# A decode step of attention and SwiGLU on one core: the loop over KV groups gets a ninth pass, both K blocks of a group go ahead of the V blocks, and most of the output projections use 512-column matmuls

## The chip, the cores and the metric

The kernel runs on one core of a Trainium2 chip. The metric is the device time of one execution in microseconds (us). Three runs gave 354.53, 354.72 and 354.78 us; the median is 354.72 us.

The core's engines run side by side and wait for each other on semaphores: TensorE (PE in the profile; PEld is its weight load), VectorE (DVE), ScalarE (ACT), GpSimd (POOL), and SyncE (SP), which here only issues transfers. Transfers from memory run on 16 DMA engines that the SP queue feeds.

## The reference

One token of width 512 goes through two branches, and a gate mixes them.

```python
q = (x @ wq)                                  # 32 heads of 128
k = repeat(k_cache, 4); v = repeat(v_cache, 4)  # 8 KV heads, 32768 keys of 128
p = softmax(q . k * 128 ** -0.5)
a = (p @ v).reshape(1, 1, 4096) @ wo          # 4096 -> 512
b = (silu(x @ w_gate) * (x @ w_up)) @ w_down  # 512 -> 1792 -> 512
g = sigmoid((x * gate_w).sum(-1))
return g * a + (1 - g) * b
```

Everything is bf16 in memory. The K and V caches are 8 x 32768 x 128 each, 67 MB apiece; wq and wo are 4.2 MB each, w_gate, w_up and w_down 1.8 MB each. Each byte of these is read once, 148 MB in all.

## The kernel before

**Tiles.** The 8 KV heads are called groups (G = 8, four query heads each). The 32768 keys of a group are cut into two blocks (NB = 2) of 16384 keys, 4 MB of K and 4 MB of V per block. On-chip memory has five pages of one block each: pages 0 and 2 take the K blocks (PG_K), pages 1 and 3 the V blocks (PG_V), page 4 (PG_X) holds wq at the start and wo at the end. Page 3 holds w_gate and w_up at first. w_down has a tile of its own, wd. This text writes K0(g), K1(g), V0(g), V1(g) for the blocks of group g.

**A K block on TensorE (emit_k, L403).** It is cut into eight units. For each unit eight fp32 transposes (L381, emit_fill) write the two PSUM tiles pst in turn; DVE copies a unit to the tile ktT (L641); 16 matmuls with the query (L393, emit_scores) write the scores to ps_sc, two units behind the transposes. After the last unit's scores DVE reduces the block's maximum (L646), and after both blocks POOL takes it over all partitions (L262). Each fill counts up sem_fill; when it has counted a whole block, that K page may be loaded anew.

**A V block on TensorE (emit_v, L428).** ACT has turned the group's scores into exponentials ET (L519). 32 matmuls with 512 columns (L440) add ET times V to ps_o, on four strips of 32 rows in turn. The last one counts up sem_v_free, and the V page is free. Ahead of block 0 stands emit_reduce (L415), eight recorded fp32 matmuls (L419) that fold the accumulator of an earlier group, which ACT copied out of PSUM (L531).

**The loop on TensorE (L450).** Eight passes, one per group. Pass g does K0(g), V0(g-1), K1(g), V1(g-1); the V blocks are skipped in pass 0. After the loop stand the V blocks of group 7, the sums of the exponentials (L470), a last emit_reduce, then w_down (emit_proj, 14 slices j with four 128-column matmuls each, one per strip), a matmul that permutes the attention output (L486), and wo (32 slices j, four matmuls each) into the same sums ps_c. DVE copies these out (L676) and SP writes the 512 outputs.

**The order of the loads (L266 on).** SP issues all large loads in one order, and a wait in front of one holds up all behind it: wq, w_gate, w_up, K0(0), K1(0), V0(0), K0(1), K1(1), V1(0), then for g from 2 to 7: K0(g), V0(g-1), K1(g), V1(g-1); then V0(7), V1(7), w_down, and wo in five cuts (WO_CUTS). Each K load waits for the fills of the block that has its page, each V load for sem_v_free of the V block that has its page. One load is different: V1(7) goes to K page 0 with a semaphore of its own (sem_vl) and waits for the fills of K0(7).

Of the kernel before, what the change touches and what calls it, by code (L numbers as in the profile page):

```python
# [13 lines left out]
def bass_gated_mix__gqa_block_cached__swiglu_ffn__decode_kernel(  # L14
# [41 lines left out]
    SCALE = float(DH) ** -0.5  # L56
    assert UPG == STEP and UPP % NKT == 0 and UPP % NST == 0
    assert KC * H * DH <= PAGE and 2 * KC * F <= PAGE and WOJ * NOUT <= PAGE
    WO_CUTS = [0, 16, 24, 28, 30, 32]
    OC = NOUT // 128  # L60

    RQ = 4
# [10 lines left out]
    with ExitStack() as es:  # L73
        def S_(name):
            return es.enter_context(nc.semaphore(name))

        sem_page = [S_(f"s_page{i}") for i in range(4)]
        sem_vl = S_("s_vl")
# [32 lines left out]
        sem_dve_oT2 = S_("s_dve_oT2")  # L111
        sem_dve_O2 = S_("s_dve_O2")
        sem_dve_row = S_("s_dve_row")
        sem_act_g = S_("s_act_g")
        sem_act_sg = S_("s_act_sg")
        sem_nbias = S_("s_nbias")
# [8 lines left out]
        def T(name, shape, dt):  # L125
            return es.enter_context(nc.sbuf_tensor(name, shape, dt))
# [42 lines left out]
        oTs = T("oTs", [128, H], BF16)  # L169
        O2a = T("O2a", [128, WOJ], BF16)  # L170
        O2 = T("O2", [128, WOJ], BF16)
        res_row = T("res_row", [128, 128], BF16)

        def P(name, shape, dt):
# [13 lines left out]

        ps_e = pst[0][:, 0:512]
        ps_c = pst[1][:, 0:512]  # L190

        def row_view(p):
            return page[:, p, :].rearrange("p (r d) -> p r d", d=DH)
# [5 lines left out]
        with nc.Block("main") as block:  # L199
# [66 lines left out]
            @block.sync  # L266
            def _(sp):
                def cache(which, g, b, p, sem):
                    sp.dma_start(  # L269
                        page[:, p, :].rearrange("p (r d) -> p r d", d=DH),  # L270
                        which[0, g, b * BLK : (b + 1) * BLK, :].rearrange("(p r) d -> p r d", r=R),
                    ).then_inc(sem, 16)

                def load_k(g, b):
                    if g:
                        sp.wait_ge(sem_fill, UPG * (g - 1) + UPP * (b + 1))
                    cache(A_k_cache, g, b, PG_K[b], sem_page[PG_K[b]])

                def load_v(g, b):
                    p, sem = PG_V[b], sem_page[PG_V[b]]  # L280
                    if (g, b) == (G - 1, NB - 1):
                        p, sem = PG_K[0], sem_vl
                        sp.wait_ge(sem_fill, UPG * (G - 1) + UPP)
                    elif g:
                        sp.wait_ge(sem_v_free, NB * (g - 1) + b + 1)
                    elif PG_V[b] == PG_F:
                        sp.wait_ge(sem_pe_h, 1)
                    cache(A_v_cache, g, b, p, sem)

                sp.dma_start(wq_v, A_wq.rearrange("(p c) n -> p c n", c=KC)).then_inc(sem_q, 16)  # L290
                for w, src in enumerate((B_w_gate, B_w_up)):
                    sp.dma_start(  # L292
                        wgu[:, w, :, :], src.rearrange("(p c) f -> p c f", c=KC)
                    ).then_inc(sem_f, 16)
                for b in range(NB):
                    load_k(0, b)
# [10 lines left out]
                sp.dma_start(  # L307
                    wd[:, :, :], B_w_down.rearrange("(p j) n -> p j n", j=FC)
                ).then_inc(sem_ld_wd, 16)
# [12 lines left out]
            @block.tensor  # L322
            def _(pe):
# [101 lines left out]
                        )  # L425
                    ins.then_inc(sem_red, 1)

                def emit_v(i, b, last=False):  # L428
                    view = row_view(PG_K[0] if last else PG_V[b])
                    if b == 0:  # L430
                        emit_reduce(i)
                    if last:
                        pe.wait_ge(sem_vl, 16)
                    else:
                        pe.wait_ge(sem_page[PG_V[b]], i)
                    pe.wait_ge(sem_exp, i + 8 * (b + 1))
                    for k in range(R // RQ):
                        n = b * R + k * RQ
                        c = k % NSTRIP
                        ins = pe.matmul(  # L440
                            ps_o[32 * c : 32 * c + RQ * HPG, :],
                            ET[:, n : n + RQ, :].rearrange("p n h -> p (n h)"),
                            view[:, k * RQ : (k + 1) * RQ, :],
                            start=(b == 0 and k < NSTRIP),
                            stop=(b == NB - 1 and k >= R // RQ - NSTRIP),
                            skip_group_check=True,
                        )
# [8 lines left out]
                def emit_proj(w, vec, j, first, last):  # L456
                    for oc in range(OC):
                        ins = pe.matmul(  # L458
                            ps_c[32 * oc : 32 * oc + 1, 0:128],
                            vec[:, j : j + 1],  # L460
                            w[:, j, oc * 128 : (oc + 1) * 128],
                            start=first,
                            stop=last,
                            skip_group_check=True,
                        )
                    return ins

                emit_v(G * STEP, 0)
                pe.wait_ge(sem_dve_esum2, 1)
                pe.matmul(  # L470
                    ps_e[:, 0:H],
                    ones_f[:, :],
                    esum2[:, :, :].rearrange("p g h -> p (g h)"),
                    start=True,
                    stop=True,
                ).then_inc(sem_pe_S, 1)
                emit_v(G * STEP, 1, last=True)
                emit_reduce((G + 1) * STEP)
                pe.wait_ge(sem_dve_tT, 1)
                pe.wait_ge(sem_ld_wd, 16)  # L480
                for j in range(FC):
                    emit_proj(wd, tT, j, j == 0, False)

                pe.wait_ge(sem_dve_oT2, 1)
                pe.wait_ge(sem_dve_pm, 1)
                pe.matmul(  # L486
                    ps_m[:, M_O0 : M_O0 + WOJ], pmat[:, :], O2a[:, :], start=True, stop=True
                ).then_inc(sem_pe_O2, 1)
                pe.wait_ge(sem_dve_O2, 1)
                for k, s in enumerate(sem_wo):  # L490
                    pe.wait_ge(s, 16)
                    for j in range(WO_CUTS[k], WO_CUTS[k + 1]):
                        ins = emit_proj(wo_v, O2, j, False, j == WOJ - 1)
                ins.then_inc(sem_pe_sum, 1)

            @block.scalar
            def _(act):
# [44 lines left out]
            def _(dve):  # L542
# [162 lines left out]
```

## Time and profile before

| | |
|---|---|
| median of three runs | 354.72 us |
| the profiled execution | 354.56 us, of which the span 352.8 us |
| mean granted TensorE clock | 0.848 of full speed |
| busy: PE, PEld, DVE, ACT, POOL | 268.0, 233.3, 176.5, 32.3, 5.8 us |
| DMA | 148.26 MB, 420 GB/s over the span |
| K load, V load (16 each) | 4096 KB, 27.7 and 31.5 us from issue to landing (median) |
| SP waited for TensorE's transposes | 215.8 us in 14 waits |
| SP waited for TensorE's V matmuls | 75.0 us in 13 waits |

How to read it: the profile is of one execution. Time from issue to landing holds the time that a load stands in the queue behind earlier loads. SP's waits are not a cost in themselves: SP has nothing else to do. A line of the timeline gives start, length, engine, line, operation, tile written and tiles read, the count, and in square brackets the idle time before it with what ended it. Matmul ends are modelled.

### The profile page before, as it was taken

What the parts mean: (1) busy time and instruction counts of PE and PEld (TensorE: products, weight loads), DVE (VectorE), ACT (ScalarE), POOL (GpSimd) and SP (SyncE); (2) the same over time, 40 slices, a digit from 0 to 9 for tenths busy, and PEclk for the clock granted to TensorE, in tenths of its full rate; (3) what the DMA queues carried; (4) which work ended last, traced back from release to release, by engine and by line L of the source; (5) the groups of instructions that cost most, each with busy time, mean ns of one, the idle gap of its engine ahead of it and who ended that gap; (6) DMA issues with size and microseconds to landing.
All of it is one profiled execution on the core that took longest, in us unless ns stands there. A gap on an engine that the chain in (4) does not pass through costs nothing.

```text
span 352.8 us, 8863 instructions
## 1 busy us (share of the span) xinstructions
PE 268.0 (76%) x4093; PEld 233.3 (66%) x4093; DVE 176.5 (50%) x201; ACT 32.3 (9%) x148; POOL 5.8 (2%) x24
## 2 busy tenths in 40 slices
PE   0446986999897949796796959894997949695584
PEld 0446986978796939494775739593967849494243
DVE  1210977566692818375564719083654818192000
ACT  1000000400300040003000030004000030004000
POOL 0200000000000000000000000000000000000000
PEclk9999989698998987789898879589785978898655
DMA  8999999999999999999999999999999999999994
GB/s 327 414 432 433 440 422 404 431 427 438 431 431 424 446 428 424 424 450 427 427 424 450 424 427 427 446 424 427 427 446 424 427 436 435 431 424 438 408 423 165
DMA packets 5926, 148.26 MB, mean 420 GB/s; under 512 B 666, under 2 KB 668, under 8 KB 1052
## 3 DMA queue, kind: packets, MB, share of 16 engines
q1 hardware_dynamic: 5912, 148.12, 98.1%
q8 instruction: 7, 0.11, 0.1%
q14 instruction: 3, 0.02, 0.0%
q10 hardware_dynamic: 4, 0.00, 0.0%
HBM read 148.11 MB, written 0.00 MB: 420 GB/s over the span
## 4 chain that ended last, share of the span: by engine, by line
DMA 65%; PE 31%; DVE 2%; SPq 1%; issue 0%
DMA page<-in_A_k_cache_dram 53%; PE pst L381 23%; DMA page<-in_A_wo_dram 12%; PE ps_sc L393 5%; PE ps_o L440 2%; DVE ktT L641 2%; PE ps_m L419 1%; SPq L314 0%; SPq L292 0%; SPq L269 0%; SPq L307 0%; PE pst L458 0%; SPq L290 0%; DVE res_row L676 0%
## 5 line engine op out<-in xcount | busy, mean ns | idle before, releaser
L641 DVE COPY ktT<-pst 128x2048 bf16<-128x2048 bf16 x128 | 156.0, 1224 | 110.1 <-PE pst L381 103.1
L381 PE MATMUL pst<-ident_f,page 128*128 128x128 f32 x1024 | 158.7, 313 | 43.5 <-DMA page<-in_A_k_cache_dram 41.6
L381 PEld LDWEIGHTS pst<-ident_f,page 128*128 128x128 f32 x1024 | 135.8, 162 | 54.0 <-DMA page<-in_A_k_cache_dram 49.4
L393 PEld LDWEIGHTS ps_sc<-qcur,ktT 128*128 128x128 bf16 x2048 | 67.0, 97 | 11.4 <-DVE ktT L641 10.0
L393 PE MATMUL ps_sc<-qcur,ktT 128*128 128x8 bf16 x2048 | 67.8, 166 | 8.6 <-DVE ktT L641 8.6
L440 PE MATMUL ps_o<-page,ET 128*16 128x512 bf16 x512 | 41.3, 480 | 5.0 <-DMA page<-in_A_v_cache_dram 5.0
L440 PEld LDWEIGHTS ps_o<-page,ET 128*16 128x16 bf16 x512 | 13.2, 103 | 22.1 <-issue 9.9
L510 ACT ACTIVATE nbias<-gmax 128x4 f32<-128x4 f32 x8 | 1.6, 205 | 263.8 <-POOL gmax L262 263.8
L519 ACT ACTIVATE ET<-ps_sc,nbias 128x128 bf16<-128x128 f32 x64 | 24.1, 552 | 0.9 <-PE ps_o L440 0.3
L519 ACT ACTIVATION_READ_ACCUMULATOR ET<-ps_sc,nbias 128x1 f32 x64 | 18.0, 281 | 0.0
L646 DVE TENSOR_REDUCE pmaxf<-ps_sc 128x4 f32<-128x512 f32 x16 | 11.1, 692 | 10.4 <-PE ps_sc L393 10.4
L419 PE MATMUL ps_m<-sel,acc 128*128 128x4 f32 x72 | 11.6, 284 | 4.1 <-ACT acc L531 4.1
L419 PEld LDWEIGHTS ps_m<-sel,acc 128*128 128x128 f32 x72 | 10.9, 232 | 5.5 <-ACT acc L531 5.5
L366 PE MATMUL ps_m<-xT,page 128*128 128x1 bf16 x112 | 6.9, 198 | 5.2 <-DMA page<-in_B_w_up_dram 5.2
L366 PEld LDWEIGHTS ps_m<-xT,page 128*128 128x128 bf16 x112 | 6.8, 162 | 5.3 <-DMA page<-in_B_w_up_dram 5.3
L262 POOL PARTITION_ALL_REDUCE gmax<-pmax x8 | 3.0, 374 | 293.0 <-DVE pmax L648 293.0
L632 DVE COPY oT<-ps_m 128x4 f32<-128x4 f32 x8 | 1.3, 156 | 12.9 <-PE ps_m L419 12.9
L342 PE MATMUL ps_m<-xT,page 128*128 128x1 bf16 x128 | 3.6, 165 | 5.3 <-DMA page<-in_A_wq_dram 5.3
L342 PEld LDWEIGHTS ps_m<-xT,page 128*128 128x128 bf16 x128 | 3.5, 104 | 5.3 <-issue 5.3
L531 ACT ACTIVATE acc<-ps_o 128x512 f32<-128x512 f32 x8 | 5.2, 649 | 14.6 <-PE ps_o L440 14.6
L329 PE MATMUL ps_m<-ones_bf,x_row 1*128 1x1 bf16 x4 | 0.3, 172 | 7.8 <-DMA gw_row<-in_gate_w_dram 7.8
L458 PE MATMUL pst<-page,O 128*1 128x128 bf16 x128 | 4.3, 305 | 2.5 <-DMA page<-in_A_wo_dram 2.4
(62 smaller groups left out, 24.0 us busy)
## 6 DMA issues: line engine op xcount, KB each, us to landing
page<-in_A_k_cache_dram SPq DMA_DIRECT2D x16, 4096.0 KB, 27.7
page<-in_A_v_cache_dram SPq DMA_DIRECT2D x16, 4096.0 KB, 31.5
page<-in_A_wq_dram SPq DMA_DIRECT2D x1, 4096.0 KB, 12.7
page<-in_A_wo_dram SPq DMA_DIRECT2D x1, 2048.0 KB, 39.7
page<-in_B_w_gate_dram SPq DMA_DIRECT2D x1, 1792.0 KB, 16.5
page<-in_B_w_up_dram SPq DMA_DIRECT2D x1, 1792.0 KB, 21.3
wd<-in_B_w_down_dram SPq DMA_DIRECT2D x1, 1792.0 KB, 35.3
page<-in_A_wo_dram SPq DMA_DIRECT2D x1, 1024.0 KB, 41.8
```

The source lines that it names most:

```text
L262: pool.partition_all_reduce(gmax[:, g, :], pmax[:, g, :], 128, ReduceOp.max).then_inc(sem_gmax, 1)
L342: ins = pe.matmul(ps_m[:, M_Q0 + h : M_Q0 + h + 1], wq_v[:, c, h * DH : (h + 1) * DH], xT[:, c : c + 1], start=(c == 0), stop=(c == KC - 1),)
L366: ins = pe.matmul(ps_m[:, base + j : base + j + 1], wgu[:, w, c, :].rearrange("d (p j) -> d j p", j=FC)[:, j, :], xT[:, c : c + 1], start= ...
L381: ins = pe.transpose(pst[u % NST][:, k * 128 : (k + 1) * 128], kv[:, n * 128 : (n + 1) * 128], ident_f[:, :],)
L393: ins = pe.matmul(ps_sc[b][:, col : col + 2 * HPG], kt[:, k, e, :], qcur[:, e, :], start=(e == 0), stop=(e == 1),)
L419: ins = pe.matmul(ps_m[:, M_P0 : M_P0 + HPG], acc[:, q, :], sel4[:, q * HPG : (q + 1) * HPG], start=(q == 0), stop=(q == RQ - 1),)
L440: ins = pe.matmul(ps_o[32 * c : 32 * c + RQ * HPG, :], ET[:, n : n + RQ, :].rearrange("p n h -> p (n h)"), view[:, k * RQ : (k + 1) * RQ, ...
L458: ins = pe.matmul(ps_c[32 * oc : 32 * oc + 1, 0:128], vec[:, j : j + 1], w[:, j, oc * 128 : (oc + 1) * 128], start=first, stop=last, skip_ ...
L519: act.activation(ET[:, b * R : (b + 1) * R, h], sc[:, h, :], ACT.Exp, bias=nbias[:, g, h : h + 1], scale=SCALE, accum_out=esum[:, g, b, h ...
L531: act.activation(acc[:, :, :].rearrange("p q d -> p (q d)"), ps_o[:, :], ACT.Copy).then_inc(sem_acc, STEP)
L641: dve.tensor_copy(ktT[:, u % NKT, :], pst[u % NST][:, :].bitcast(BF16)).then_inc(sem_cp, 1)
L646: dve.tensor_reduce(pmaxf[:, f, :], sc, AX.X, ALU.max).then_inc(sem_pmax, 1)
```

## The change

Three edits go together.

1. On TensorE the loop has nine passes. Pass i does K0(i) and K1(i) if i < 8, then V0(i-1) and V1(i-1) if i > 0, and, if i is 8, the code that stood behind the loop (emit_end). In pass 8 the sums of the exponentials come after V1(7), no longer between V0(7) and V1(7).
2. SP issues, for g from 2 on, K0(g), K1(g), V0(g-1), V1(g-1). V1(7) goes to its ordinary page 3 and waits like the others for sem_v_free (that of V1(6)); sem_vl is gone.
3. w_down's 14 slices and the first 20 of wo are multiplied by one 512-column matmul each (emit_wide), slice j on strip j mod 4 of a new PSUM region ps_w, which DVE clears beforehand. DVE copies ps_w to the tile part, and four fp32 matmuls with the selector sel4 add its strips to ps_c. The last 12 slices of wo stay with four 128-column matmuls each (emit_rows). The cuts of wo are now 20, 6, 3, 2 and 1 slices, before 16, 8, 4, 2 and 2.

```diff
-    WO_CUTS = [0, 16, 24, 28, 30, 32]
+    WO_CUTS = [0, 20, 26, 29, 31, 32]
...
+        part = T("part", [128, NOUT], FP32)
...
+        ps_w = pst[0][:, 512:1024]
...
                 def load_v(g, b):
-                    p, sem = PG_V[b], sem_page[PG_V[b]]
-                    if (g, b) == (G - 1, NB - 1):
-                        p, sem = PG_K[0], sem_vl
-                        sp.wait_ge(sem_fill, UPG * (G - 1) + UPP)
-                    elif g:
+                    if g:
                         sp.wait_ge(sem_v_free, NB * (g - 1) + b + 1)
                     elif PG_V[b] == PG_F:
                         sp.wait_ge(sem_pe_h, 1)
-                    cache(A_v_cache, g, b, p, sem)
+                    cache(A_v_cache, g, b, PG_V[b], sem_page[PG_V[b]])
...
                 for g in range(2, G):
                     for b in range(NB):
                         load_k(g, b)
+                    for b in range(NB):
                         load_v(g - 1, b)
...
-                def emit_v(i, b, last=False):
-                    view = row_view(PG_K[0] if last else PG_V[b])
+                def emit_v(i, b):
+                    view = row_view(PG_V[b])
                     if b == 0:
                         emit_reduce(i)
-                    if last:
-                        pe.wait_ge(sem_vl, 16)
-                    else:
-                        pe.wait_ge(sem_page[PG_V[b]], i)
+                    pe.wait_ge(sem_page[PG_V[b]], i)
...
-                with pe.Fori(0, G * STEP, STEP) as i:
-                    for b in range(NB):
-                        emit_k(i, b)
-                        with pe.If(i > 0):
-                            emit_v(i, b)
...
+                def emit_wide(w, vec, j, first, last):
+                    c = j % NSTRIP
+                    return pe.matmul(
+                        ps_w[32 * c : 32 * c + 1, :],
+                        vec[:, j : j + 1],
+                        w[:, j, :],
+                        start=first,
+                        stop=last,
+                        skip_group_check=True,
+                    )
+
+                def emit_rows(lhs, rhs, first, last):
                     for oc in range(OC):
                         ins = pe.matmul(
                             ps_c[32 * oc : 32 * oc + 1, 0:128],
-                            vec[:, j : j + 1],
-                            w[:, j, oc * 128 : (oc + 1) * 128],
+                            lhs,
+                            rhs[:, oc * 128 : (oc + 1) * 128],
...
+                def emit_end():
+                    pe.wait_ge(sem_dve_esum2, 1)
...
+                    emit_reduce((G + 1) * STEP)
+                    pe.wait_ge(sem_dve_tT, 1)
+                    pe.wait_ge(sem_ld_wd, 16)
+                    pe.wait_ge(sem_psw, 1)
+                    for j in range(FC):
+                        emit_wide(wd, tT, j, j < NSTRIP, False)
...
+                    for k, s in enumerate(sem_wo):
+                        pe.wait_ge(s, 16)
+                        for j in range(WO_CUTS[k], WO_CUTS[k + 1]):
+                            if k == 0:
+                                ins = emit_wide(wo_v, O2, j, False, j >= WO_CUTS[1] - NSTRIP)
+                            else:
+                                ins = emit_rows(
+                                    O2[:, j : j + 1], wo_v[:, j, :], j == WO_CUTS[1], j == WOJ - 1
+                                )
+                        if k == 0:
+                            ins.then_inc(sem_pe_w, 1)
+                        if k == 1:
+                            pe.wait_ge(sem_dve_w, 1)
+                            emit_rows(sel4[:, 0:1], part[:, :], False, False)
+                    ins.then_inc(sem_pe_sum, 1)
+
+                with pe.Fori(0, (G + 1) * STEP, STEP) as i:
+                    with pe.If(i < G * STEP):
+                        for b in range(NB):
+                            emit_k(i, b)
+                    with pe.If(i > 0):
+                        for b in range(NB):
+                            emit_v(i, b)
+                    with pe.If(i > (G - 1) * STEP):
+                        emit_end()
...
+                dve.memset(ps_w[:, :], 0.0).then_inc(sem_psw, 1)
                 copy_red(G - 2)
...
+                dve.wait_ge(sem_pe_w, 1)
+                dve.tensor_copy(part[:, :], ps_w[:, :]).then_inc(sem_dve_w, 1)
```

More of the change, by code (lines that the diff above doesn't have):

```diff
@@ L77, in bass_gated_mix__gqa_block_cached__swiglu_ffn__decode_kernel @@
         sem_page = [S_(f"s_page{i}") for i in range(4)]
-        sem_vl = S_("s_vl")
         sem_q = S_("s_q")
@@ L113, in bass_gated_mix__gqa_block_cached__swiglu_ffn__decode_kernel @@
         sem_dve_row = S_("s_dve_row")
+        sem_psw = S_("s_psw")
+        sem_pe_w = S_("s_pe_w")
+        sem_dve_w = S_("s_dve_w")
         sem_act_g = S_("s_act_g")
@@ L448, in emit_v @@
                     ins.then_inc(sem_v_free, 1)
-                with pe.Fori(0, G * STEP, STEP) as i:
-                    for b in range(NB):
-                        emit_k(i, b)
-                        with pe.If(i > 0):
-                            emit_v(i, b)
-                def emit_proj(w, vec, j, first, last):
+                def emit_wide(w, vec, j, first, last):
[9 more added lines that the diff above has]
+                def emit_rows(lhs, rhs, first, last):
                     for oc in range(OC):
@@ L466, in emit_proj @@
                     return ins
[L468 to L493, printed above, removed]
@@ L494, in _ @@
-                ins.then_inc(sem_pe_sum, 1)
+                def emit_end():
+                    pe.wait_ge(sem_dve_esum2, 1)
+                    pe.matmul(
+                        ps_e[:, 0:H],
+                        ones_f[:, :],
+                        esum2[:, :, :].rearrange("p g h -> p (g h)"),
+                        start=True,
+                        stop=True,
+                    ).then_inc(sem_pe_S, 1)
+                    emit_reduce((G + 1) * STEP)
[4 more added lines that the diff above has]
+                        emit_wide(wd, tT, j, j < NSTRIP, False)
+                    pe.wait_ge(sem_dve_oT2, 1)
+                    pe.wait_ge(sem_dve_pm, 1)
+                    pe.matmul(
+                        ps_m[:, M_O0 : M_O0 + WOJ], pmat[:, :], O2a[:, :], start=True, stop=True
+                    ).then_inc(sem_pe_O2, 1)
+                    pe.wait_ge(sem_dve_O2, 1)
+                    for k, s in enumerate(sem_wo):
[13 more added lines that the diff above has]
+                    ins.then_inc(sem_pe_sum, 1)
```

## The prediction

> **What bounds the kernel now.** I read the page's slices and DMA queues first, then the chain that ended last, then SP's own timeline and the tensor engine's in the last group.
>
> ```profile
> PE 268.0 (76%) x4093; PEld 233.3 (66%) x4093; DVE 176.5 (50%) x201; ACT 32.3 (9%) x148; POOL 5.8 (2%) x24
> ...
> DMA  8999999999999999999999999999999999999994
> ...
> q1 hardware_dynamic: 5912, 148.12, 98.1%
> ...
> DMA 65%; PE 31%; DVE 2%; SPq 1%; issue 0%
> ```
>
> The SP queue's transfers fill 98.1% of the span and no slice between the first and the last falls under nine tenths; no engine is that full. The kernel is one stream of 148 MB, and TensorE stands in the chain only where it releases a page for a later load. So the question is whether a load is ever issued after the queue has run out. SP's timeline tells when each load of the last group was issued:
>
> ```profile
> 258.98 0.33 SPq L269 DMA_DIRECT2D page<-in_A_k_cache_dram  x1
> 264.74 0.33 SPq L269 DMA_DIRECT2D page<-in_A_v_cache_dram  x1
> 278.75 0.33 SPq L269 DMA_DIRECT2D page<-in_A_k_cache_dram  x1
> 282.48 22.17 SPq L269 DMA_DIRECT2D page<-in_A_v_cache_dram  x3
> 304.69 0.43 SPq L307 DMA_DIRECT2D wd<-in_B_w_down_dram  x1
> ```
>
> These are K0, V0(6), K1 of group 7, and in the merged row V1(6) at 282.48 with V0(7) and V1(7), which the chain puts at 303.84 and 304.22. I write V0(6) for block 0 of group 6's V. When the data arrives is read from the tensor engine's timeline:
>
> ```profile
> 287.14 5.38 PE L381 MATMUL pst<-ident_f,page 128*128 128x128 f32 x24 [4.71 <-DMA page<-in_A_k_cache_dram]
> ...
> 300.52 0.56 PE L393 MATMUL ps_sc<-qcur,ktT 128*128 128x8 bf16 x16 [0.54 <-DVE ktT L641]
> ...
> 300.93 1.03 PE L419 MATMUL ps_m<-sel,acc 128*128 128x4 f32 x8
> ...
> 301.89 1.90 PE L440 MATMUL ps_o<-page,ET 128*16 128x512 bf16 x32
> ...
> 306.54 4.50 PE L381 MATMUL pst<-ident_f,page 128*128 128x128 f32 x24 [2.74 <-DMA page<-in_A_k_cache_dram]
> ...
> 335.71 3.59 PE L440 MATMUL ps_o<-page,ET 128*16 128x512 bf16 x32 [4.96 <-DMA page<-in_A_v_cache_dram]
> ...
> 350.00 0.38 PE L458 MATMUL pst<-page,O 128*1 128x128 bf16 x8 [0.28 <-DMA page<-in_A_wo_dram]
> ```
>
> K0(7) lands at 287.10 and K1(7), two 4 MB loads later, at 306.50: one load takes 9.70 us of stream. V1(6) then lands at 316.2, V0(7) at 325.9, V1(7) at 335.6 (seen: 335.71), the rest by 350.0. V0(7) was issued at 303.84, 12.4 us before the load ahead of it landed: the stream never ran dry.
>
> **Load order, passes 1 to 6.** After the change TensorE does K0, K1, V0, V1 in a pass, and SP issues in that order. Time t counts from K0's landing. K0 takes 13.9 us on TensorE (287.14 to 301.08), with its last transposes at t+12.1. K1 directly behind it has two rows: 46.16 to 59.53 in pass 0 (13.4 us, the granted clock 0.50 from 47.5 to 50.5), and 94.36 to 106.24 behind a V block (11.9 us). I take 12.6, so K1 ends at t+26.5. Then the reduction and V0: over passes 1 to 7 from the last score to V0's release it took 2.8 to 5.0 us (2.8 at 301.08 to 303.84; 5.0 at 221.17 to 226.20 with a clock of 0.50), mean 3.7; V0 ends at t+30.2. V1 lands at t+29.1 and ends by t+33. The period is 38.8 us, so the next K0, issued at t+12, is needed at t+29; the next K1, issued at t+25, at t+39; V0, issued at t+30, at t+48. Every margin is over 13 us. Tightest is K1 of group 2, early on: it waits for K1(1)'s transposes, now 76.30 + 10.0 to 12.0 = 86.3 to 88.3, and the load ahead of it lands at 91.7 (K0(3), four loads later, lands at 130.55). I take 0 here; if the 2 us that an issue needs were not covered, it would cost about 0 to 1 us. Exponentials: ACT's eight take 2.8 us and are done by t+36, before the next scores. Cost 0, hidden by the stream.
>
> **The last group, where the cost is.** V0(7) is no longer followed by K loads. It waits for V0(6) to be released, and behind it on SP stand V1(7), w_down and all of wo. V1(7) also loses its early slot in K page 0 (its old wait, K0(7)'s transposes, was over by 299.2) and now waits for V1(6). V0(6) no longer runs between K0 and K1 but after both: 301.08 + 12.6 (K1) + 3.7 (reduction and V0) = 317.4, in place of 303.84. From the rows' ends it is 301.08 + 11.9 + 2.8 = 315.8 at the earliest and 301.08 + 13.4 + 5.0 = 319.5 at the latest. V1(6) lands at 316.2, and then nothing is queued.
>
> How long from issue to landing on an empty queue? Two rows. wq, the same 4 MB, was issued at 0.73 into an empty queue and used at 13.55: 12.8 us, with the start's other transfers beside it. The output's 1 KB, issued at 350.76, is waited for until about 352.4 (0.62 of issue, then SP's wait of 1.0): 1.6 us of fixed cost, and with 9.7 of stream 11.3. I take 12.0, the middle. V0(7) lands at 317.4 + 12.0 = 329.4 in place of 325.9: **+3.5 us**, with ends 315.8 + 11.3 - 325.9 = +1.2 and 319.5 + 12.8 - 325.9 = +6.4. All later loads shift by the same amount, since V1(7), released near 321, follows while V0(7) still streams. Nothing after 316 can win it back: V1(7), wd and wo are 24 us of stream.
>
> On first bytes: wq's issue began at 0.73 and packets show from 1.6, so 0.9 us. The Trainium skill (DMA: Bandwidth & Descriptors, "Latency and other measured facts") gives about 0.6 us to the first byte for loads issued by SP. An estimate from that page, 317.4 + 0.6 against a queue dry near 315.7, would be +2.3 instead of +3.5.
>
> **The tail.** The stream's end is called E (350.0 before); 1 of the 32 wo slices is 0.32 us of it (1.28 us from 347.4 to 348.68 for four). Added on DVE: a memset of 512 columns (0.49, the row of L608) after esum2, in an idle stretch of over 2 us: 0. The S matmul (0.55) moves behind V1(7), beside ACT's accumulator copy (0.60 to 0.66): 0. w_down by 14 wide matmuls: a row of four strips at 512 columns cost 3.59/32 = 0.112 us per matmul at clock 0.50, so 1.6 us where 56 narrow ones took 1.66: 0. O2 is then ready at E-6.1 as now. The first wo cut (20 slices) lands at E-3.9; 20 x 0.112 = 2.2, done at E-1.65. DVE's copy of ps_w is bounded by 0.49 (memset) and 0.69 (L646's reduction of 512 columns): at 0.65 it ends at E-0.9, with 24 narrow matmuls (0.03 each, 1.88/64) beside it. The four fp32 matmuls have no row: two fp32 instructions of 32 columns took 0.55, and 24 fp32 transposes 5.38, 0.22 each; I take 0.55, ends 0.3 and 1.8. They end at E-0.3, and the last 24 matmuls (0.7) and the drain bring E+0.65, where the old tail needed E+0.41. **+0.3 us**, from -0.1 (only four matmuls behind the last landing) to +1.3.
>
> **Branches.** A pass now has three tests and in pass 8 a jump over all of the K code. In the trace the skip in pass 0 cost 0.42 us of idle time at 46.58, all inside slack; new jumps fall where TensorE waits for a load (59.5 to 62.5; 321 to 329). I take 0. The Trainium skill (Runtime: NRT & Kernel Launch, "Instruction fetch mechanics") speaks against it: a taken branch out of the fetched window waits for a fetch. [...]
>
> **Rivals.** (1) The queue never dries. V0(6) would have to end by 325.9 - 11.3 = 314.6, which needs K1 and V0 in 13.5 us; the fastest rows add to 14.7. Only the tail is left: 354.6 to 355.0, not slower. For it: K1's data lies ready, so its start is warm. Against it: no pass of the trace is that quick. (2) The last group is late as said, and a second hole opens: code fetched late or K1(2) issued too late. POOL's unexplained waits of 10 to 11 us early on (L212, L257) bound such a fetch; a stall of 3 to 7 us in pass 0 would use up K1(2)'s slack and cost 1 to 5 more: 359.5 to 363.5. Against it: TensorE shows no such gap at its own first entry into V code. (3) The hole opens and is smaller than 0.7 us, because late engines of the 16 (from 348.0 on only about one moves bytes) set the landing while the others refill: 355.0 to 355.4.
>
> **How the numbers follow.** Span 352.8 + 3.5 + 0.3 = 356.6; the profiled execution was 354.56, 1.76 outside the span, so 358.4; it stands 0.16 below the median of 354.72, and I keep 358.4. The likeliest case has 0.76, (2) 0.09, (1) 0.08, (3) 0.07. A measurement of this kernel tells about 0.2%, 0.7 us, from no change. Slower by more: 0.76 + 0.09, and 0.02 of (3) = 0.87; within: 0.09; faster: 0.04, from (1) with a shorter tail than any row. The range runs from 355.6 (+1.2 and -0.1) to 361.6 (short of the upper ends of both terms, +6.4 and +1.3, which would need every slow row at once).
>
> **What would show it.** SP's wait for ps_o before V0(7) ends at 316 to 319.5, the DMA share drops for 1 to 4 us just there and nowhere else, V1(7)'s matmuls start at 337 to 342, and the last wo cut's at 351 to 356. If the share stays at nine tenths through 320, the main step is wrong; if it drops near 90, the early margin was.

## The result and the profile after

The changed kernel took 357.71 us in the median of 15 runs (355.35 to 358.76), the kernel before 354.72 us (353.87 to 355.78). The ratio is 1.0066, with a 95% interval of 1.0043 to 1.0089: the change makes the kernel slower by about two thirds of a per cent. The runs fall into two clusters, six at 355.35 to 356.38 and nine at 357.64 to 358.76. The profiled execution is of the upper one: 358.76 us, span 357.0 us, 4.2 us more than the span before.

The page of the changed kernel, lines that answer to those shown of before, and the bytes per slice:

```profile
PE 252.9 (71%) x3999; PEld 218.6 (61%) x3999; DVE 177.8 (50%) x203; ACT 33.5 (9%) x148; POOL 5.8 (2%) x24
...
DMA  8999999999999999999999999999999999949995
GB/s 334 406 422 457 417 417 443 424 422 437 430 422 448 422 427 444 422 426 448 419 430 452 411 437 444 411 441 441 411 441 441 408 444 437 415 158 415 416 442 229
...
q1 hardware_dynamic: 5912, 148.12, 97.1%
...
DMA 61%; PE 35%; DVE 3%; SPq 1%; issue 1%
```

The same 148.12 MB move, and 38 of the 40 slices show the same DMA share as before. The last one has five tenths instead of four. The other is slice 36 (each is 8.9 us, so this is 312 to 321): it falls from nine tenths to four and moves 158 GB/s, where slice 36 of before had 424. That is the hole. The same place by stretches (length, busy time and count of PE, PEld, DVE, ACT and POOL, then granted clock, DMA share, GB/s), first the kernel before, then the changed kernel:

```profile
312.00:318.00 6.00, 6.00 (x116) 5.94 (x115) 5.59 (x6) 0.00 (x0) 0.00 (x0) 1.00 1.02 437
```

```profile
304.00:312.00 8.00, 7.80 (x157) 7.64 (x154) 7.51 (x7) 0.00 (x0) 0.00 (x0) 1.00 1.03 442
312.00:318.00 6.00, 5.66 (x60) 3.24 (x64) 1.29 (x4) 0.21 (x1) 0.37 (x1) 0.58 0.17 71
318.00:320.00 2.00, 2.00 (x24) 0.67 (x20) 0.00 (x0) 1.61 (x8) 0.00 (x0) 0.55 0.93 262
```

From 312 to 318 the queue moves 71 GB/s in place of 437. TensorE is busy all through that stretch, 5.66 of 6 us, but at a mean clock of 0.58. What it was doing, and when SP could issue again (timelines of the changed kernel, SP's first):

```profile
258.87 12.11 SPq L273 DMA_DIRECT2D page<-in_A_k_cache_dram  x2
275.27 45.75 SPq L273 DMA_DIRECT2D page<-in_A_v_cache_dram  x4
321.06 0.44 SPq L308 DMA_DIRECT2D wd<-in_B_w_down_dram  x1
```

```profile
317.97 3.06 SPq L273 DMA_DIRECT2D page<-in_A_v_cache_dram  x2
```

```profile
287.33 5.34 PE L382 MATMUL pst<-ident_f,page 128*128 128x128 f32 x24 [8.71 <-DMA page<-in_A_k_cache_dram]
...
312.34 0.56 PE L394 MATMUL ps_sc<-qcur,ktT 128*128 128x8 bf16 x16 [0.54 <-DVE ktT L663]
312.75 1.65 PE L420 MATMUL ps_m<-sel,acc 128*128 128x4 f32 x8
314.33 6.31 PE L438 MATMUL ps_o<-page,ET 128*16 128x512 bf16 x64
...
330.40 3.39 PE L438 MATMUL ps_o<-page,ET 128*16 128x512 bf16 x32 [6.02 <-DMA page<-in_A_v_cache_dram]
340.12 3.59 PE L438 MATMUL ps_o<-page,ET 128*16 128x512 bf16 x32 [6.33 <-DMA page<-in_A_v_cache_dram]
```

The merged SP row starts at 275.27 with V0(6) and V1(6) and ends 45.75 us later with V0(7) and V1(7); the row of the narrower window puts the issue of V0(7) at 317.97, where the kernel before had 303.84. K0(7) landed at 287.29 (before 287.10), so the stream had lost only 0.2 us up to there. V0(7) is used at 330.40 and V1(7) at 340.12, 4.41 us later than the 335.71 of before, and the span is 4.2 us longer. After V1(7) nothing has grown: 16.9 us to the end, before 17.1.

### The profile page after: what moved, and what is told of

Read it like the earlier page. It is cut to its first block, busy times and chain, and to the rows that moved or that the text cites. A ratio compares the mean times of both kernels' runs of the same rounds, so it can differ in the third digit from the quotient of the medians.

```text
span 357.0 us, 8699 instructions
## 1 busy us (share of the span) xinstructions
PE 252.9 (71%) x3999; PEld 218.6 (61%) x3999; DVE 177.8 (50%) x203; ACT 33.5 (9%) x148; POOL 5.8 (2%) x24
## 3 DMA queue, kind: packets, MB, share of 16 engines
q1 hardware_dynamic: 5912, 148.12, 97.1%
## 4 chain that ended last, share of the span: by engine, by line
DMA 61%; PE 35%; DVE 3%; SPq 1%; issue 1%
DMA page<-in_A_k_cache_dram 52%; PE pst L382 24%; DMA page<-in_A_wo_dram 8%; PE ps_sc L394 6%; DVE ktT L663 3%; PE ps_o L438 3%; PE ps_m L420 1%; PE pst L450 1%; PE pst L461 0%; SPq L292 0%; DVE part L699 0%; SPq L308 0%; SPq L290 0%; SPq L273 0%; DVE res_row L701 0%
## 5 line engine op out<-in xcount | busy, mean ns | idle before, releaser
L382 PE MATMUL pst<-ident_f,page 128*128 128x128 f32 x1024 | 147.7, 297 | 48.9 <-DMA page<-in_A_k_cache_dram 44.8
L382 PEld LDWEIGHTS pst<-ident_f,page 128*128 128x128 f32 x1024 | 124.4, 153 | 54.8 <-DMA page<-in_A_k_cache_dram 47.9
L438 PE MATMUL ps_o<-page,ET 128*16 128x512 bf16 x512 | 39.7, 471 | 18.8 <-DMA page<-in_A_v_cache_dram 17.3
L541 ACT ACTIVATE ET<-ps_sc,nbias 128x128 bf16<-128x128 f32 x64 | 25.3, 546 | 24.2 <-PE ps_o L438 24.1
L668 DVE TENSOR_REDUCE pmaxf<-ps_sc 128x4 f32<-128x512 f32 x16 | 11.1, 692 | 10.4 <-PE ps_sc L394 10.4
## 6 DMA issues: line engine op xcount, KB each, us to landing
page<-in_A_wq_dram SPq DMA_DIRECT2D x1, 4096.0 KB, 12.8
```

Source lines behind the costliest of these rows:

```text
L382: ins = pe.transpose(pst[u % NST][:, k * 128 : (k + 1) * 128], kv[:, n * 128 : (n + 1) * 128], ident_f[:, :],)
L438: ins = pe.matmul(ps_o[32 * c : 32 * c + RQ * HPG, :], ET[:, n : n + RQ, :].rearrange("p n h -> p (n h)"), view[:, k * RQ : (k + 1) * RQ, ...
L541: act.activation(ET[:, b * R : (b + 1) * R, h], sc[:, h, :], ACT.Exp, bias=nbias[:, g, h : h + 1], scale=SCALE, accum_out=esum[:, g, b, h ...
L668: dve.tensor_reduce(pmaxf[:, f, :], sc, AX.X, ALU.max).then_inc(sem_pmax, 1)
```

## The experiments

All times are medians beside runs of the kernel before on the same chip (354.43 to 354.53 us). The theory was that only the late issue of V0(7) costs; the rivals were the order of K and V as such, the ninth pass with its jumps, and the wide tail.

**V0(7) early, the rest of the change kept.**

```diff
-                    if g:
+                    p, sem = PG_V[b], sem_page[PG_V[b]]
+                    if (g, b) == (G - 1, 0):
+                        p, sem = PG_K[0], sem_vl
+                        sp.wait_ge(sem_fill, UPG * (G - 1) + UPP)
+                    elif g:
...
+                        with pe.If(i > 0):
+                            emit_v(i, 0)
+                    with pe.If(i > (G - 1) * STEP):
+                        emit_v(i, 0, last=True)
                     with pe.If(i > 0):
-                        for b in range(NB):
-                            emit_v(i, b)
+                        emit_v(i, 1)
```

> The changed kernel, but V0(7) goes to K page 0 as soon as K0(7)'s transposes have read it (near 299), as V1(7) did in the kernel before; V1(7) still waits for V1(6), and the order, the nine passes and the wide tail stay. Theory (the queue runs dry between V1(6) and V0(7)): the DMA share stays near 1.0 from 305 to 345, V1(7) is used near 335.7 to 336.0 instead of 340.1, and of the added time only the tail's 0.2 to 0.5 us is left: span 353.0 to 353.4, time 354.8 to 355.3. The spread between runs shrinks to that of the kernel before. Rival (the ninth pass, its jumps or the tail cost it): the time stays at 357 to 358. Rival (the order of K and V slows the stream everywhere): V1(7) is still used near 340.

Measured: 357.46 us (357.18 to 358.27), ratio 1.0075 (1.0056 to 1.0094). As a time this is a miss. The profile shows two things. The hole of the last group is gone: 421 GB/s from 312 to 318. But a new one stands at the start, where pass 0 ends and the loop goes back (timelines of TensorE and SP, then stretches):

```profile
57.31 0.56 PE L399 MATMUL ps_sc<-qcur,ktT 128*128 128x8 bf16 x16 [0.40 <-DVE ktT L674]
69.00 3.24 PE L387 MATMUL pst<-ident_f,page 128*128 128x128 f32 x14 [11.14 <-issue]
```

```profile
80.98 12.11 SPq L274 DMA_DIRECT2D page<-in_A_k_cache_dram  x2
```

```profile
76.00:80.00 4.00, 4.00 (x76) 3.97 (x74) 3.73 (x4) 0.00 (x0) 0.00 (x0) 1.00 0.86 369
80.00:84.00 4.00, 3.46 (x69) 3.36 (x68) 3.02 (x4) 0.00 (x0) 0.00 (x0) 1.00 0.61 188
84.00:92.00 8.00, 7.56 (x129) 7.26 (x128) 7.59 (x7) 0.00 (x0) 0.00 (x0) 1.00 0.99 430
92.00:98.00 6.00, 5.46 (x83) 4.00 (x85) 2.84 (x5) 0.21 (x1) 0.37 (x1) 0.73 0.74 268
```

TensorE stood still for 11.14 us from 57.9 to 69.0, with nothing that the profile could name as the releaser, although K0(1) had landed by 62.7 in the changed kernel. K0(2), which waits for K0(1)'s transposes, was issued at 80.98 (74.54 in the changed kernel), K1(2) near 92.8, and the stream dropped at each: 188 GB/s from 80 to 84, 268 from 92 to 98. V1(7) was used at 339.05, near the 340 that the last rival gave. But the delay was there before the last group: K0(7) was used at 290.36, 3.2 us later than before, and from there to V1(7) it took 48.7 us, where the kernel before took 48.6 and the changed kernel 52.8. So this edit, which adds a second copy of V0's code to TensorE's loop, took one hole away and opened another. A form without the second one comes below.

**V0(7) later.**

```diff
-                        sp.wait_ge(sem_v_free, NB * (g - 1) + b + 1)
+                        sp.wait_ge(sem_v_free, NB * (g - 1) + b + 1 + (1 if (g, b) == (G - 1, 0) else 0))
```

> The changed kernel with one wait raised: V0(7) is issued only when V1(6), too, is released. In the changed kernel's profile V0(6) was released at 317.9 and V1(6) at 320.7. Theory: the hole grows by just that, 2.3 to 2.8 us, and with it the time, slope 1: V1(7) used near 342.5 to 343, time 359.5 to 361.5, mean 2.3 to 2.8 above the changed kernel's. Rival (the hole is partly caught up later, or the end is set by something else): less than 1.5 us added.

Measured: 359.73 us (359.26 to 360.90, four runs), ratio 1.0132 (1.0108 to 1.0156), 2.0 us above the changed kernel's median and 2.7 above its mean of 357.17 (mean 359.91). In its profile V0(7) was issued at 319.97 and used at 332.24, V1(7) at 341.95 (342.5 to 343 was expected), and the span was 359.1. Against the profile above the issue is 2.0 us later, V1(7) 1.8 and the span's end 2.1, so the slope is 1 within the noise. No run lies where the lower cluster was. That was to be expected: in the profile of that cluster, shown below, V1(6) was released at 317.7, 3.6 us after V0(6), which by the same slope puts the lower cluster (355.6 in the mean) near 359.2, an estimate. Four runs do not tell whether there are still two clusters.

**The old order, the rest of the change kept.**

```diff
-                    with pe.If(i < G * STEP):
-                        for b in range(NB):
-                            emit_k(i, b)
-                    with pe.If(i > 0):
-                        for b in range(NB):
-                            emit_v(i, b)
+                    for b in range(NB):
+                        with pe.If(i < G * STEP):
+                            emit_k(i, b)
+                        with pe.If(i > 0):
+                            emit_v(i, b)
...
                         load_k(g, b)
-                    for b in range(NB):
                         load_v(g - 1, b)
```

> The changed kernel with the old order K0, V0, K1, V1 put back on TensorE and in the loads; nine passes, all later code in the loop, the wide tail, and V1(7) on its ordinary page (waiting for V1(6)) stay. Theory: V0(7) is issued near 304 again and V1(7) near 321, over 3 us before the queue would run out at 325.9; no hole, time 354.8 to 355.3, and so neither the loop form nor V1(7)'s page costs anything. Rival (loop form, jumps): 357 to 358. Rival (V1(7)'s lost early slot makes the hole): a hole near 326 and 355.5 to 357.

Measured: 354.65 us (354.13 to 356.40, 12 runs), ratio 1.0000 (0.9986 to 1.0013). V1(7) was used at 336.14, and the stream ran at 393 to 459 GB/s through 318 to 332, so there is no hole near 326 either. The ninth pass, the wide tail and V1(7) on its ordinary page cost nothing that can be told from none, together. The loss needs the new order.

**The old tail, the rest of the change kept.**

```diff
-    WO_CUTS = [0, 20, 26, 29, 31, 32]
+    WO_CUTS = [0, 16, 24, 28, 30, 32]
...
-                                ins = emit_wide(wo_v, O2, j, False, j >= WO_CUTS[1] - NSTRIP)
+                            ins = emit_rows(O2[:, j : j + 1], wo_v[:, j, :], False, j == WOJ - 1)
```

> The changed kernel with the old projections put back inside the ninth pass: w_down and wo by four 128-column matmuls each and the old cuts 16, 8, 4, 2, 2; no ps_w, no copy, no fp32 matmuls. Theory: the hole stays as it is (V1(7) used at 337 to 340), only the tail's +0.2 to +0.5 us goes: 0.2 to 0.5 us under the changed kernel, so a time of 355.0 to 358.5 with the same two clusters. Rival (the wide tail makes up most of the loss): 355 in all runs.

Measured: 357.86 us (357.07 to 359.88), ratio 1.0085 (1.0061 to 1.0108). Not a gain of 0.2 to 0.5 us, and no run under 357. Its profile has the late hole (V0(7) issued at 319.08, V1(7) used at 341.07) and the early one too: K0(1) began at 67.75 after 9.14 us put down to issue. These are two effects at once, but the rows part them. K0(7) was used at 288.96, 1.8 us later than before, and from there to V1(7) it took 52.1 us, 3.5 more than before. From V1(7)'s use to the end took 17.0 us, with the wide tail 16.9 and in the kernel before 17.1. So the wide tail is not the loss; what it adds or saves is under what the runs can tell.

**The order alone on the kernel before, with V0(7) early.** Eight passes, later code behind the loop, old tail; so no extra instructions in the loop.

```diff
-                if (g, b) == (G - 1, NB - 1):
+                if (g, b) == (G - 1, 0):
...
                         load_k(g, b)
+                    for b in range(NB):
                         load_v(g - 1, b)
...
                         emit_k(i, b)
-                        with pe.If(i > 0):
+                    with pe.If(i > 0):
+                        for b in range(NB):
                             emit_v(i, b)
...
-                emit_v(G * STEP, 0)
+                emit_v(G * STEP, 0, last=True)
...
-                emit_v(G * STEP, 1, last=True)
+                emit_v(G * STEP, 1)
```

> The kernel before with only the new order (K0, K1, V0, V1 on TensorE, K, K, V, V in the loads); the special K page goes to V0(7) instead of V1(7); eight passes, the later code behind the loop and the old tail stay. So the order is tried without the late issue of V0(7) and without the jump over later code that held K0(1) to 69.0 in the run with V0(7) early (57.9 to 69.0, put down to issue, after which the DMA share fell at 80 and at 94). Theory (only V0(7)'s late issue costs in the new order): V0(7) issued near 299, no hole at 313 to 320 or at 80, V1(7) used near 335.7; time 354.4 to 355.0, no change from before. Rival (the order in itself costs, through K1(2)'s thin margin near 88 or through the stream): a drop of the share near 90, 355.5 to 358.

Measured: 354.63 us (354.07 to 355.31, 12 runs), ratio 1.0004 (0.9995 to 1.0012). The new order costs nothing that can be told from none when V0(7) is issued in time. Here it was issued at 299.41, and V1(7) was used at 335.91. V0(7)'s issue on SP (V1(7)'s is merged with it), then the same stretches as above, now of this kernel:

```profile
299.41 20.09 SPq L269 DMA_DIRECT2D page<-in_A_v_cache_dram  x2
```

```profile
304.00:312.00 8.00, 7.94 (x158) 7.78 (x156) 7.50 (x7) 0.00 (x0) 0.00 (x0) 1.00 1.03 442
312.00:318.00 6.00, 5.52 (x72) 2.97 (x76) 1.44 (x4) 0.68 (x4) 0.37 (x1) 0.72 1.02 437
318.00:320.00 2.00, 1.12 (x24) 0.28 (x12) 0.00 (x0) 1.89 (x13) 0.00 (x0) 1.00 0.88 377
```

From 312 to 318 TensorE is nearly as busy as in the changed kernel, 5.52 us, and its clock falls here too, to a mean of 0.72 against 0.58, but the stream runs through at 437 GB/s.

**The order alone, both V blocks of group 7 on their ordinary pages.** It differs from the last kernel in the page of V0(7), and so in what its load waits for:

```diff
-                if (g, b) == (G - 1, 0):
+                if False:
...
-                emit_v(G * STEP, 0, last=True)
+                emit_v(G * STEP, 0)
```

> The same with V0(7) and V1(7) both on their ordinary pages, as in the changed kernel; eight passes, later code behind the loop, old tail. It differs from the run with V0(7) early in that one page. Theory: the hole of 313 to 318 is there without the ninth pass and without the wide tail; the time lies where the changed kernel's runs lie less 0 to 0.4 us: 355.2 to 358.5, mean 356.5 to 357.5. Rival (the hole needs the ninth pass, whose jump over the K code delays V0(7)): 354.4 to 355.0.

Measured: 356.74 us (356.29 to 360.28), ratio 1.0094 (1.0058 to 1.0130). The loss is back without the ninth pass and without the wide tail. This pair is the cleanest of the study: one page apart, 2.1 us in the medians, 3.0 in the means (357.65 and 354.64). V0(7)'s issue and first use, and the same stretch as above:

```profile
314.33 3.75 SPq L269 DMA_DIRECT2D page<-in_A_v_cache_dram  x2
```

```profile
327.88 3.41 PE L441 MATMUL ps_o<-page,ET 128*16 128x512 bf16 x32 [6.89 <-DMA page<-in_A_v_cache_dram]
```

```profile
312.00:318.00 6.00, 4.18 (x68) 1.76 (x68) 0.60 (x3) 1.99 (x10) 0.37 (x1) 1.00 0.67 235
```

The profiled execution (356.55 us), with the clock at 1.00 in this stretch, is one of four at 356.29 to 356.92. The two highest runs, 359.41 and 360.28, lie above the 358.5 that was expected, as the mean lies above its 357.5; no profile shows what those two were.

**The jump alone.** The old order, the ninth pass and the old tail inside it. The loop against that of the kernel before:

```diff
-                with pe.Fori(0, G * STEP, STEP) as i:
-                    for b in range(NB):
-                        emit_k(i, b)
-                        with pe.If(i > 0):
-                            emit_v(i, b)
...
+                with pe.Fori(0, (G + 1) * STEP, STEP) as i:
+                    for b in range(NB):
+                        with pe.If(i < G * STEP):
+                            emit_k(i, b)
+                        with pe.If(i > 0):
+                            emit_v(i, b)
+                    with pe.If(i > (G - 1) * STEP):
+                        emit_end()
```

> The old order of K and V, with the ninth pass and the old tail inside it, so that the loop's end lies 392 instructions further from the V code's end than in the kernel before. Theory (code behind the jump in pass 0 comes late: the fewer instructions there, the shorter the wait; 5.4 us of idle time in the changed kernel, 9.1 with the old tail, 11.1 with V0(7) early): K0(1)'s first transposes begin near 68 to 70 instead of 62.5, K0(2) is issued near 80 to 82 instead of 74.5, the share drops there for up to 2 us, and the time is 355.2 to 357.0 although the last group has no hole. Rival (the late start came from the K, K order): the transposes begin at 62.5 to 63.5 and the time is 354.4 to 355.0.

Measured: 355.07 us (354.33 to 357.31, 10 runs), ratio 1.0021 (1.0005 to 1.0038). The wait is there:

```profile
67.51 4.74 PE L381 MATMUL pst<-ident_f,page 128*128 128x128 f32 x21 [8.62 <-issue]
```

K0(2) was issued at 79.51, and the stream fell to 311 GB/s from 80 to 82. In the old order that costs 0.05 to 0.4%, a little less than was expected (355.07 against 355.2 and more); the profiled execution (354.52 us, K0(7) used at 287.10) shows that it can also cost nothing. In the new order a late K0(1) hits K0(2) and K1(2) both, as in the first experiment. In the changed kernel TensorE was idle there for 5.38 us, put down to K0(1)'s DMA, and went on at 63.13, 0.4 us after those data were there, so what the jump took was covered to within 0.4 us.

**The changed kernel again.**

> The changed kernel once more, for its spread and a second profile. Its 15 runs fell into two clusters, 355.4 to 356.4 and 357.6 to 358.8. Theory (the granted clock in the last reduction and V0(6) sets when V0(7) is issued): if the profiled run is of the upper cluster, the clock falls to 0.50 before V0(6) ends and V0(7) is issued at 317 to 318.5; if of the lower one, the clock stays 1.00 through V0(6), V0(7) is issued at 315.5 to 316.3, and V1(7) is used near 337. Rival (the clusters come from the jump in pass 0): V0(7) is issued at the same time after K0(7) in both, and they differ near 60 to 100.

Measured: 355.02, 355.45, 355.99, 357.98, 358.29 and 358.48 us, the two clusters again. The profiled execution is the fastest, so there is a profile of each cluster:

```profile
311.14 1.03 PE L420 MATMUL ps_m<-sel,acc 128*128 128x4 f32 x8
...
312.11 1.90 PE L438 MATMUL ps_o<-page,ET 128*16 128x512 bf16 x32
314.06 3.94 SPq L273 DMA_DIRECT2D page<-in_A_v_cache_dram  x2
...
326.35 1.03 PE L438 MATMUL ps_o<-page,ET 128*16 128x512 bf16 x8 [5.13 <-DMA page<-in_A_v_cache_dram]
```

```profile
304.00:312.00 8.00, 7.46 (x154) 7.33 (x151) 6.91 (x7) 0.00 (x0) 0.00 (x0) 1.00 1.05 451
312.00:314.00 2.00, 2.00 (x34) 0.79 (x33) 0.34 (x3) 0.21 (x1) 0.37 (x1) 1.00 0.42 180
314.00:315.00 1.00, 0.01 (x3) 0.00 (x0) 0.00 (x0) 0.85 (x5) 0.00 (x0) 1.00 0.00 0
315.00:316.00 1.00, 0.28 (x8) 0.17 (x12) 0.00 (x0) 0.74 (x6) 0.00 (x0) 1.00 1.90 524
```

Here the clock is 1.00 through the reduction and V0(6): 2.8 us for both, where the upper cluster's profile took 5.1 at 0.50. V0(7) was issued at 314.06, before the 315.5 to 316.3 that was expected and 3.9 us earlier than in the upper cluster; V1(7) was used at 336.07, 4.05 us earlier, and the span is 353.2, 3.8 us shorter. Of the 3.9 us the clock in these two operations explains 2.3; K0(7) landed 0.8 us earlier, and K0's transposes took 0.8 less, with the clock at 0.65 against 0.50 in the first of them (286.5 to 291 here, 287 to 292.5 there). From K0(7)'s first use to V0(7)'s issue it is 27.6 us against 30.6, so the rival, by which this stretch is the same in both, does not hold. That the clock makes the clusters is read from these two profiles and was not forced by an edit. The mean clock of a whole run does not show it: it is 0.858 to 0.884 in the nine runs of the lower cluster and 0.856 to 0.876 in the twelve of the upper one.

**The reduction behind V0.** The wait for ACT's copy stays ahead of V0, because both use ps_o; only the matmuls move.

```diff
                     if b == 0:
+                        pe.wait_ge(sem_acc, i)
+                    else:
                         emit_reduce(i)
```

> The changed kernel with the reduction's matmuls between V0 and V1 in place of ahead of V0; the wait for ACT's copy stays ahead of V0. So V0(6) ends earlier by the reduction's length, 0.9 us (clock 1.00) to 1.5 us (clock 0.50), and nothing else moves. Theory (the time follows V0(7)'s issue, also downwards): V0(7) issued near 313.1 or 316.5, used 12.3 us later, lower cluster at 354.4 to 355.0, which is the kernel before, upper cluster at 356.5 to 357.2; the median 0.9 to 1.5 us under the changed kernel's. Rival (something else than V0(7)'s issue sets the end): no change, 357 to 358.

Measured: 355.56 us (354.42 to 357.53, 12 runs), ratio 1.0041 (1.0022 to 1.0060): 2.2 us under the changed kernel's first median, 1.4 under the second. There are still two clusters, seven runs at 354.42 to 355.58 and five at 356.74 to 357.53. Their means (355.04 and 357.11) lie 0.6 and 1.1 us under those of the changed kernel's 21 runs (355.60 and 358.20), a little less than expected. More of the runs are in the lower one. In the profile V0(7) was issued at 314.68, between the two values that were expected, and used at 327.22: V0(6) ran at the full clock, but K0's first transposes took 5.38 us, as in the upper cluster (5.34), and not 4.38, as in the lower one.

**The order with V0(7) early and a smaller last cut.**

```diff
-    WO_CUTS = [0, 16, 24, 28, 30, 32]
+    WO_CUTS = [0, 16, 24, 28, 31, 32]
```

> The new order with V0(7) in K page 0 (eight passes, old tail, no hole, as run before at 354.63), with wo's last two cuts at 3 and 1 slices, so that four in place of eight matmuls stand behind the last landing. Theory (one stream of transfers bounds the time and only what stands behind the last landing is left): 0.0 to 0.15 us under the kernel before, 354.3 to 354.6, within what can be told from no change. Rival (the new order gives the stream something): more than 0.7 us under.

Measured: 354.33 us (354.08 to 354.73, 11 runs), ratio 0.9997 (0.9988 to 1.0006). No difference from the kernel before that can be told; no version was found that beats it.

**The dose, over all profiles with a hole in the last group.** The first two rows, without a hole, are for comparison. When V0(7) was issued, when K0(7), V0(7) and V1(7) were used, and the span:

| kernel | K0(7) used | V0(7) issued | V0(7) used | V1(7) used | from K0(7) to V1(7) | span |
|---|---|---|---|---|---|---|
| before | 287.14 | 303.84 | 326.68 | 335.71 | 48.6 | 352.8 |
| order alone, V0(7) early | 287.28 | 299.41 | 326.21 | 335.91 | 48.6 | 353.0 |
| changed, lower cluster | 286.50 | 314.06 | 326.35 | 336.07 | 49.6 | 353.2 |
| order alone, ordinary pages | 286.65 | 314.33 | 327.88 | 337.62 | 51.0 | 354.7 |
| reduction behind V0 | 287.11 | 314.68 | 327.22 | 336.84 | 49.7 | 353.7 |
| changed, upper cluster | 287.33 | 317.97 | 330.40 | 340.12 | 52.8 | 357.0 |
| old tail | 288.96 | 319.08 | 331.35 | 341.07 | 52.1 | 358.1 |
| V0(7) later | 286.55 | 319.97 | 332.24 | 341.95 | 55.4 | 359.1 |

From 314.06 to 319.97 is 5.9 us of issue, and the span grows by 5.9. With a hole, issue to use is 12.3 to 12.5 us in five of the six (13.6 in the other), and V1(7) to the end is 16.9 to 17.2 us in all eight. The column from K0(7) to V1(7) is the last group by itself: 48.6 us without a hole, 1.0 to 6.8 us more with one.

## Why the prediction was right, step by step

**Direction and size.** 358.4 us was forecast, 357.71 is the median, and the profiled execution is 358.76. The likeliest case is the one that happened in nine of 15 runs. The other six are at 355.35 to 356.38, three of them under the low end of 355.6. The prediction has one value around 358 and not two clusters; that more than half of these 15 runs fell into the upper one, and the median with them, is luck. In the six later runs it was three and three, with a median of 356.98, and then the sum would have been 1.4 us too high.

**V0(7) is issued late (317.4, ends 315.8 and 319.5).** Right: 317.97 in the upper cluster. That it is so close is in part luck, for two terms erred against each other. K1 directly behind K0 took 11.8 us in both profiles and not 12.6: the row of pass 0, with its fall of the clock, was the wrong end to average in. The reduction with V0(6) took 5.1 and not the mean 3.7. The lower end was set too high: in the lower cluster's profile K0, K1, the reduction and V0 took 27.6 us from K0's landing, where the fastest rows had added to 28.7, and K0(7) landed 0.6 us earlier than before. Of the 1.1 us, 0.9 lie in K0 (13.0 us in place of 13.9). Rival (1) had fixed K0's end at 301.08 and asked whether K1, the reduction and V0 can take 13.5 us; they took 14.6, so its words that no pass is that quick still hold. V0(7) went out before its mark of 314.6 all the same, and the queue ran dry: no byte moved from 314 to 315.

**Issue to landing on an empty queue (12.0, ends 11.3 and 12.8).** Right: 12.3 to 12.5, one 13.6. The first packets of V0(7) show 0.9 to 1.0 us after its issue in both profiles of the changed kernel (from 318.9 and from 315.0), like the 0.9 read from wq's row.

**The step itself (+3.5).** +4.4 at V1(7) in the upper cluster, inside the ends given (+1.2 and +6.4), and +0.4 in the lower one, 0.8 under the low end. There the hole itself made 1.0 us, and the earlier K0(7) took 0.6 off. So the step came as two values rather than as one around 3.5.

**The tail (+0.3).** Mis-sized: it is 0. From V1(7)'s use to the end took 17.1 us before, 16.9 and 17.1 after, and the old-order run shows a ratio of 1.0000 with this tail. Over six profiles with the wide tail the mean is 17.06 us, over five with the old one 17.05. The terms were not far off (20 wide matmuls 2.30 us against 2.2, the copy 0.70 against 0.65, the four fp32 matmuls 0.51 and 0.60 against 0.55). The last 24 matmuls took 0.60 us where it is 16.9 and 0.86 where it is 17.1 or 17.2; 0.7 had been taken. The last landing is not seen separately in the wide tail, so which term makes up the missing 0.3 us stays open.

**Early margin of K1(2) (0).** Right for the change as it stands; the share stays at nine tenths from 80 to 100. The margin is as thin as it was said to be: where K0(1) was late by 6 us, both the next K loads left the queue short.

**Branches (0).** Right as a price, by little. The row that was used, 0.42 us for a skip over one V block, said nothing of a jump over more code. In the changed kernel the jump's place shows 5.4 us of idle time, nearly all of it the wait for K0(1); in three other kernels with the ninth pass it was 8.6 to 11.1 us, of which up to 6.3 were not covered. Rival (2), a second hole early on, did not come about in the changed kernel and did in those; K0(7) was later by 3.2 us in the first experiment and by 1.8 with the old tail. The Trainium skill (Runtime: NRT & Kernel Launch, "Instruction fetch mechanics") says that a taken branch out of the fetched window has to wait for a fetch, in units of 256 instructions. The DMA records fit that in part. In the changed kernel one packet of an instruction queue (q8, 0.02 MB) shows in the idle time, between 59.5 and 60, and the next between 65.5 and 66, when TensorE has gone on; the kernel before has the first of the two. In the three with the long wait two show before TensorE goes on, the second between 64 and 66, and TensorE goes on about 3 us behind it (2.7 to 3.5). The records do not say whose instructions a packet holds, and no run changed the packets alone, so the wait is shown and its cause is not.

## What to carry to other kernels

In a kernel that one stream of transfers bounds, look at the last rounds of a reordered loop by themselves: loads that were issued between others for the whole loop have nothing ahead of them at its end, and then the next landing comes a whole issue-to-landing time after the release of a buffer (here 12.3 us for a 4 MB load, against 9.7 in a full queue). A spare buffer that is free early belongs to the load whose release comes last relative to its turn, which a change of order can move to another load. A loop whose body skips code on its first pass should be looked at in the profile at that point, since a wait that is covered by a transfer in one form of the code may not be in the next.

## What was not expected of the hardware

The granted clock fell to 0.50 while TensorE was working. In the changed kernel's first profile no gap from 300 to 318 was longer than 0.54 us, the clock was 1.00 from 300 to 312, and from 313 to 318 TensorE was busy all the time, with fp32 reductions and matmuls of 16 weight columns, at 0.50. In another execution of the same kernel the same operations ran at 1.00, behind a gap of the same length. Where such a step decides when a load is issued, it shows in the time of the whole kernel: here 2.3 us of the 3.9 us between the two issues. Also, the DMA queue does not stop at once: from 313 to 315, when the rest had stopped, 0.07 MB in 12 packets still moved (33 GB/s, the work of about one of the 16 engines).
